# Linear attention with an MLP behind it: k turned by VectorE and DRAM, masks by ScalarE and GpSimd, TensorE in stated order

## The chip, the cores and the metric

The kernel runs on one core of a Trainium2 chip. The metric is the device time of one execution in microseconds, as a median of several executions. No run here fell in a slower state: each profile names the mean granted clock of TensorE, 0.97 to 1.00 of full speed in all of them, 0.995 before and 0.994 after.

## The reference, cut to what matters

```python
def _attn_ref(q, k, v, alpha):                     # (4, 8, 768, 48) each
    for t in range(S):
        state = alpha[:, :, t, :, None] * state + einsum('bhd,bhe->bhde', k[:, :, t], v[:, :, t])
        y[:, :, t] = einsum('bhd,bhde->bhe', q[:, :, t], state)

def _moe_ref(x, w_in, w_out):                      # 3072 tokens, 384 -> 2048 -> 384
    h = x @ w_in
    return (h * (1.0 / (1.0 + exp(-h)))) @ w_out   # x is y, heads side by side
```

## The kernel before: what the change and the argument touch

TensorE makes all matrix products here. They land in PSUM, in pieces called banks, from which ScalarE or VectorE has to take them before a bank can be used again. GpSimd does small work on the side, and SyncE issues DMAs.

The attention is done in 24 chunks of 128 tokens (6 per batch). In each, decayed k and q give scores, the scores are masked, masked scores and the state give values, and k with v gives the next state. The first 8 chunks are done with little beside them. In the 16 "late" ones, from the ninth on, the MLP's products of earlier tokens stand between the steps of a chunk; I call these *dense*. They use a scheme with fewer products and more sums, and the sums are VectorE's. VectorE also reads all weights and alpha once to prove that the scheme is safe; I call that the *guard*.

The late chunk, in the order of its stages (scores of the chunk before, then products, values and states, quotient):

```python
stages = [[(scores, 1)], [(products, 0)], [(values, 1), (states, 1)], [(quotient, 0), (blank, 0)]]

def scores(n):
    ps = c.pop("blank") if n >= NA else [ps_attn() for _ in range(2)]    # zeroed by ScalarE when late
    ...                                              # 32 products of 64 rows, the upper halves only
    for u in range(2):
        if n < NA:  ...                              # early: ScalarE copies, GpSimd selects
        m = mask[:, :, None, :]                      # late: VectorE multiplies by a mask
        dve.tensor_tensor(g[:, u]..., ps[u]..., m.to_broadcast(...), ALU.mult)
    if ci < NCH - 1:
        ps_k = ps_attn()
        for j in range(NP):
            pe.transpose(ps_k[:, j, :], c["kp"][:, j, :], ident)         # k for the state product
        c["kn"] = work.tile([128, NP, C], F32, name="kn")
        act.copy(c["kn"], ps_k)
```

Two more places carry the argument. `enter` makes the dense products of the first layer in three banks of PSUM; a bank is free again when ScalarE has copied it or VectorE has added it (`tt`), and the next product waits for that:

```python
def enter(grp, pair):
    ...
    add(a); tt(s[4], a, s[4])                        # VectorE frees bank a
```

`audit`, the guard, has one buffer: load, reduce for the maximum, reduce for the minimum (for the weights), next load, with VectorE's reductions kept in a stated order.

## Time and profile before

| kernel before | |
|---|---|
| time, median of the 3 runs made before the prediction | 561.52 us (561.36 to 562.27) |
| span of the profiled execution | 559.1 us |
| last product of TensorE ends at | 553.76 us |
| TensorE's waits after 127 us | two, 0.4 and 0.3 us |
| VectorE busy, 130 to 294 us | 145.6 of 164 us |
| VectorE busy, 450 to 517 us | 45.8 of 67 us |

The rows from which TensorE's and VectorE's load is read are in the prediction. The last two show where VectorE has room and where not. That the last stage has some did not make it safe, as the runs show.

### The profile page before, as it was taken

How to read it: one execution, taken by the hardware profiler on the slowest of the kernel's cores; microseconds unless marked ns; L12 is line 12 of the kernel's file. 1: busy time of each engine (PE TensorE's matmuls, PEld its weight loads, DVE VectorE, ACT ScalarE, POOL GpSimd, SP SyncE). 2: the span in 40 equal slices, each digit the busy share in tenths (PEclk: the TensorE clock that was granted, in tenths of full speed). 3: DMA queues.
4: the chain of work that ended last, by engine and by line, in shares of the span. 5: the costliest groups of instructions: out<-in, count | busy, mean ns of one | idle time of the engine just before them, and what ended most of it. 6: DMA issues, size and time to landing. Idle time of an engine off the chain costs nothing.

```text
span 559.1 us, 12435 instructions
## 1 busy us (share of the span) xinstructions
PE 543.4 (97%) x5074; PEld 492.6 (88%) x5074; DVE 448.1 (80%) x821; ACT 208.9 (37%) x414; POOL 20.8 (4%) x44
## 2 busy tenths in 40 slices
PE   5999999999999999999999999999999999999996
PEld 3788887898999999899989999999898999999995
DVE  5887789956998799986998897899895885857731
ACT  3456653323233342442433442443443342332100
POOL 5110000300000000000000000000000000000000
PEclk9899999999999999999999999999999999999999
DMA  9999871143443333333425444435422123334200
GB/s 208 223 288 201 235 187 42 26 118 100 101 107 97 82 86 88 98 87 86 130 69 162 141 113 133 131 81 154 132 69 88 53 84 118 101 98 122 72 30 26
DMA packets 94417, 63.81 MB, mean 114 GB/s; under 512 B 55312, under 2 KB 86032, under 8 KB 94352
## 3 DMA queue, kind: packets, MB, share of 16 engines
q1 hardware_dynamic: 94352, 62.94, 43.2%
q8 instruction: 41, 0.67, 0.5%
q14 instruction: 24, 0.20, 0.1%
HBM read 58.20 MB, written 4.72 MB: 113 GB/s over the span
## 4 chain that ended last, share of the span: by engine, by line
PE 79%; DVE 12%; DMA 3%; ACT 2%; SPq 1%; issue 1%; POOL 0%; DVEq 0%; ACTq 0%
PE ps_o L982 35%; PE ps_m L884 21%; PE ps_m L860 11%; PE ps_a L802 6%; PE ps_a L759 3%; PE ps_a L776 2%; DMA qn<-in_q_dram 1%; DVE g L898 1%; DMA bits<-in_moe_w_in_dram 1%; DVE u L701 1%; PE ps_a L817 1%; DVE p L730 1%; DVE seen L665 1%; SPq L456 1%; DVE w_out L626 1%
## 5 line engine op out<-in xcount | busy, mean ns | idle before, releaser
L982 PE MATMUL ps_o<-w_out,g 128*128 128x192 f32 x768 | 133.6, 328 | 0.0
L982 PEld LDWEIGHTS ps_o<-w_out,g 128*128 128x128 f32 x768 | 125.5, 190 | 2.7 <-issue 0.6
L982 PE MATMUL ps_o<-wt,g 128*128 128x192 f32 x576 | 100.0, 327 | 0.0
L982 PEld LDWEIGHTS ps_o<-wt,g 128*128 128x128 f32 x576 | 95.1, 190 | 1.5
L860 PE MATMUL ps_m<-xt,w_in 128*128 128x256 f32 x384 | 88.3, 382 | 0.8 <-ACT xt L807 0.8
L860 PEld LDWEIGHTS ps_m<-xt,w_in 128*128 128x128 f32 x384 | 71.1, 190 | 10.6 <-ACT xt L807 1.2
L884 PE MATMUL ps_m<-xc,w_in 128*128 128x256 f32 x288 | 70.1, 379 | 0.0
L884 PEld LDWEIGHTS ps_m<-xc,w_in 128*128 128x128 f32 x288 | 54.0, 190 | 6.4 <-DVE g L898 0.2
L665 DVE TENSOR_REDUCE seen<-bits 128x1 f32<-128x384 int32 (+2 forms) x65 | 42.4, 689 | 15.1 <-DMA bits<-in_moe_w_out_dram 14.9
L895 ACT ACTIVATE g<-g 128x1024 f32<-128x1024 f32 x32 | 33.1, 1055 | 56.5 <-DVE g L898 56.5
L987 DVE TENSOR_TENSOR g<-g 128x512 f32<-128x512 f32 x72 | 48.4, 685 | 6.0 <-PE ps_o L982 5.9
L890 ACT COPY g<-ps_m 128x512 f32<-128x512 f32 x64 | 36.7, 586 | 36.1 <-PE ps_m L884 36.0
L884 PE MATMUL ps_m<-xc,wx 128*128 128x256 f32 x192 | 50.1, 383 | 0.0
L782 ACT ACTIVATE st<-st,least 128x96 f32<-128x96 f32 x80 | 24.1, 364 | 57.3 <-DVE least L704 57.3
L884 PEld LDWEIGHTS ps_m<-xc,wx 128*128 128x128 f32 x192 | 35.0, 190 | 4.2 <-issue 0.4
L898 DVE TENSOR_TENSOR g<-ps_m,g 128x512 f32<-128x512 f32 x56 | 37.3, 681 | 0.7 <-PE ps_m L884 0.5
L701 DVE TENSOR_TENSOR_SCAN u<-al,one 128x516 f32<-128x516 f32 x24 | 29.1, 1211 | 8.7 <-POOL mask L535 4.5
L730 DVE TENSOR_TENSOR_SCAN p<-al,inv 128x516 f32<-128x516 f32 x24 | 29.4, 1225 | 5.2 <-PE ps_a L802 4.9
L863 ACT ACTIVATE g<-ps_m 128x512 f32<-128x512 f32 x32 | 19.0, 594 | 38.7 <-PE ps_m L860 38.6
L802 PE MATMUL ps_a<-g,vn 128*32 128x128 f32 x768 | 27.9, 281 | 1.8 <-POOL g L766 1.7
L802 PEld LDWEIGHTS ps_a<-g,vn 128*32 128x32 f32 x768 | 20.4, 111 | 9.1 <-issue 5.6
L890 ACT COPY part<-ps_m 128x512 f32<-128x512 f32 x32 | 18.6, 582 | 21.8 <-PE ps_m L884 17.6
(125 smaller groups left out, 632.1 us busy)
## 6 DMA issues: line engine op xcount, KB each, us to landing
bits<-in_moe_w_in_dram SPq DMA_DIRECT2D x24, 512.0 KB, 4.8
bits<-in_moe_w_out_dram SPq DMA_DIRECT2D x32, 384.0 KB, 3.3
at<-in_alpha_dram SPq DMA_DIRECT2D x64, 96.0 KB, 2.3
kt<-in_k_dram SPq DMA_DIRECT2D x64, 96.0 KB, 2.4
qt<-in_q_dram SPq DMA_DIRECT2D x64, 96.0 KB, 2.5
bits<-in_alpha_dram SPq DMA_DIRECT2D x9, 512.0 KB, 3.4
out_dram<-o SPq DMA_DIRECT2D x48, 96.0 KB, 1.7
an<-in_alpha_dram SPq DMA_DIRECT2D x8, 192.0 KB, 5.2
```

The lines of the kernel that those rows point to most:

```text
L665: dve.tensor_reduce(seen[kind][which][:, i : i + 1], x, axis=AX, op=op, apply_absolute_value=True))
L701: dve.tensor_tensor_scan(u[:, end - 1 :: -1], sg[:, end:0:-1], one[:, end:0:-1], 0.0, ALU.mult, ALU.add)
L730: dve.tensor_tensor_scan(p[:, 0:end], sg[:, 0:end], iv[:, 0:end], 0.0, ALU.mult, ALU.add)
L782: act.mul(s[:, j], s[:, j], least[:, n, j : j + 1])
L802: pe.matmul(py[32 * at : 32 * at + 32, t, :], lhsT=w, rhs=x, start=(i < 4), stop=(i >= len(todo) - 4), skip_group_check=True)
L860: pe.matmul(ps[:, e, :], lhsT=w_in[:, t, (f + e) * 128 : (f + e + 1) * 128], rhs=xt[:, t, :], start=(t == 0), stop=(t == NKT - 1))
L884: pe.matmul(ps[:, e], lhsT=block_w(w)[:, 2 * pair + e], rhs=block_x(grp, x), start=(first and e == 0), stop=(e == 1), skip_group_check=True)
L890: act.copy(to, ps)
L895: act.activation(x, x, AF.Silu)
L898: dve.tensor_tensor(to, a, b, op)
L982: pe.matmul(ps, lhsT=x, rhs=w[:, i], start=(first and i == 0), stop=(i == HF - 1), skip_group_check=True)
L987: dve.tensor_tensor(cells(grp, h, pair, *to), cells(grp, h, pair, *x), cells(grp, h, pair, *y), ALU.subtract)
```

## The change

Its intent: TensorE is the bound, so take the four transposes of k off it, and pay for the work on VectorE by taking the masks off VectorE. In parts:

1. k for the state product: VectorE transposes the 32x32 blocks (`flip`), SyncE writes the result to DRAM and reads it back with the blocks moved (`land`).
2. Masks: ScalarE copies the scores out of PSUM, GpSimd selects in place.
3. TensorE's instructions keep the order in which the program states them, from the ninth chunk on; the stages are reordered.
4. alpha, k and q are each fetched as soon as the tile is free; q's product gets a second buffer.
5. 40 of 48 output stores are issued by GpSimd.

```diff
+    def in_order(ins):
+        return tc.keep_in_program_order(ins) if late else ins
+    class pe:
+        def matmul(*args, **kw):
+            in_order(nc.tensor.matmul(*args, **kw))
 ...
-        p = turns(qps, n)
+        p = turns(qps if n < NA else [qps[0], late["p"]], n)
 ...
+    def flip(n):
+        if n < NA or c["ci"] == NCH - 1:
+            return
+        t = late["turn"].tile([128, NP, C], F32, name="turn").rearrange("p c (j d) -> p c j d", j=NP)
+        dve.transpose(t, c["kp"].rearrange("p j (c i) -> p c j i", i=32))
+        c["flip"] = dram.tile([128, NP * C], F32, name="flips")
+        nc.sync.dma_start(c["flip"], t.rearrange("p c j d -> p (c j d)"))
+    def land(n):
+        x = c.pop("flip").rearrange("(r d) (i x) -> i d r x", r=4, i=4)
+        for i in range(4):
+            nc.sync.dma_start(c["kn"][32 * i : 32 * i + 32], x[i])
 ...
-            m = mask[:, :, None, :]
-            dve.tensor_tensor(g[:, u]..., ps[u]..., m.to_broadcast(...), ALU.mult)
-        if ci < NCH - 1:
+            for u in range(2):
+                act.copy(swapped[:, :, u, :, CH:], ps[u][:, :, :, CH:])
+            for r, o in earlier:
+                for u in range(2):
+                    act.copy(swapped[r, o, u, :, 0:CH], ps[u][r, o, :, 0:CH])
+            for at, half in ((CH, later), (0, earlier)):
+                for r, o in half:
+                    gps.affine_select(x, x, pattern=[[0, NP], [1, CH]],
+                                      compare_op=ALU.is_ge, fill=0.0, base=0, channel_multiplier=-1)
+        if n < NA and ci < NCH - 1:
             ps_k = ps_attn()
 ...
-            nc.sync.dma_start(out[...], o)
+            (gps if grp < NG - 1 else nc.sync).dma_start(out[...], o)
 ...
-            stages = [[(scores, 1)], [(products, 0)], [(values, 1), (states, 1)], [(quotient, 0), (blank, 0)]]
+            stages = [[(land, 1), (scores, 1)], [(products, 0)], [(quotient, 0)],
+                      [(values, 1), (states, 1), (flip, 0)]]
```

What the diff does not show: the order of VectorE's and ScalarE's instructions is chosen by a scheduler, apart from a few that are pinned. Any edit, in the change or in an experiment, moves some of them.

More of the change, by code (lines that the diff above doesn't have):

```diff
@@ L376, in quotients, with transpose @@
     nc = tc.nc
-    pe, dve, act, gps = nc.tensor, nc.vector, nc.scalar, nc.gpsimd
+    dve, act, gps = nc.vector, nc.scalar, nc.gpsimd
+    late = {}
+    def in_order(ins):
+        return tc.keep_in_program_order(ins) if late else ins
+    class pe:
+        @staticmethod
+        def matmul(*args, **kw):
+            in_order(nc.tensor.matmul(*args, **kw))
+        @staticmethod
+        def transpose(*args):
+            in_order(nc.tensor.transpose(*args))
     B, H, S, D = q.shape
@@ L406, in quotients @@
     gpool = pool("gpool", 6)
-    opool = pool("opool", 2)
+    opool = pool("opool", 3)
     rpool = pool("rpool")
+    dram = pool("dram", 2, bass.MemoryType.DRAM)
     upool = pool("upool")
@@ L447, in quotients, with load @@
     ctxs = {}
-    def load(n):
+    def load(n, names="akq"):
+        if n == NT:
+            return
         c = ctxs.setdefault(n, dict(zip(("ci", "b"), divmod(n, B))))
@@ L452, in load @@
         for name, src in (("a", alpha), ("k", k), ("q", q)):
+            if name not in names:
+                continue
             x = src[b, :, rows, :]
@@ L517, in turns @@
     def turns(x, n):
-        return x[(n + 1) % 2 if n < NA else 0]
+        return x[(n + 1) % 2]
     one = consts.tile([128, NP * W + 1], F32, name="one")
@@ L526, in quotients @@
         gps.memset(t, 0.0)
-    mask = consts.tile([128, 2, C], F32, name="mask")
-    gps.memset(mask, 1.0)
-    for odd in range(2):
-        for e in range(2):
-            m = mask[CH * e : CH * e + CH, odd, :]
-            gps.affine_select(m, m, pattern=[[1, C]], compare_op=ALU.is_ge, fill=0.0,
-                              base=-CH * (e ^ odd), channel_multiplier=-1)
+    decayed = fix.tile([128, 2 * NP * C], F32, name="g")
+    low, high = slice(0, CH), slice(CH, C)
+    earlier, later = [(low, 0), (high, 1)], [(low, 1), (high, 0)]
+    ones = consts.tile([128, 1], F32, name="ones")
+    gps.memset(ones, 1.0)
     st = [fix.tile([128, NP, 2, D], F32, name=f"st{b}") for b in range(B)]
@@ L666, in audit @@
                                           apply_absolute_value=True))
-    xts, xcs, late = {}, {}, {}
+    xts, xcs = {}, {}
     def tokens(t):
@@ L687, in products @@
                     turned(c[name], tokens(sg))
+                    load(n + 1, "a")
                 continue
@@ L704, in products @@
         dve.tensor_single_scalar(least[:, n, :], u[:, 0:end:W], 2.0**-64, ALU.max)
-        kp = c["kp"] = turns(kps, n)
+        kp = c["kp"] = turns(kps, n) if n < NA else kps[0]
         ut = tokens(u)
@@ L709, in products @@
             turned(c["k"], ps["k"])
+            load(n + 1, "k")
         if n < NA:
@@ L734, in quotient @@
             turned(c["q"], q)
+            load(n + 1, "q")
         dve.tensor_tensor(qp, q, qp, ALU.mult)
-    def blank(n):
-        if n < NA:
+    def flip(n):
+        c = ctxs[n]
+        if n < NA or c["ci"] == NCH - 1:
             return
-        ps = ctxs[n]["blank"] = [ps_attn() for _ in range(2)]
-        for t in ps:
-            act.activation(t.rearrange("p j c -> p (j c)"), ident[:, 0:1].to_broadcast([128, 4 * C]),
-                           AF.Copy, scale=0.0)
+        t = late["turn"].tile([128, NP, C], F32, name="turn").rearrange("p c (j d) -> p c j d", j=NP)
[3 more added lines that the diff above has]
+    def land(n):
+        c = ctxs[n]
+        if "flip" in c:
+            c["kn"] = work.tile([128, NP, C], F32, name="kn")
+            x = c.pop("flip").rearrange("(r d) (i x) -> i d r x", r=4, i=4)
+            for i in range(4):
+                nc.sync.dma_start(c["kn"][32 * i : 32 * i + 32], x[i])
     def scores(n):
@@ L748, in scores @@
         ci, b = c["ci"], c["b"]
-        ps = c.pop("blank") if n >= NA else [ps_attn() for _ in range(2)]
+        ps = [ps_attn() for _ in range(2)]
         for j in (0, 2, 1, 3):
@@ L760, in scores @@
                               start=True, stop=True)
-        g = c["g"] = work.tile([128, 2, NP, C], F32, name="g")
-        for u in range(2):
-            if n < NA:
-                act.copy(g[:, u], ps[u])
-                gps.affine_select(g[:, u], g[:, u], pattern=[[0, NP], [1, C]], compare_op=ALU.is_ge,
-                                  fill=0.0, base=0, channel_multiplier=-1)
-                continue
-            m = mask[:, :, None, :]
-            dve.tensor_tensor(g[:, u].rearrange("p (o j) c -> p o j c", o=2),
-                              ps[u].rearrange("p (o j) c -> p o j c", o=2),
-                              m.to_broadcast([128, 2, NP // 2, C]), ALU.mult)
-        if ci < NCH - 1:
+        g = decayed.rearrange("p (u j c) -> p u j c", u=2, j=NP)
+        swapped = decayed.rearrange("p (o u j c) -> p o u j c", o=2, u=2, j=NP // 2)
+        c["g"] = (lambda u, j: g[:, u, j, :]) if n < NA else (
+            lambda u, j: swapped[:, j // 2, u, j % 2, :])
+        for u in range(2 if n < NA else 0):
+            act.copy(g[:, u], ps[u])
+            gps.affine_select(g[:, u], g[:, u], pattern=[[0, NP], [1, C]], compare_op=ALU.is_ge,
+                              fill=0.0, base=0, channel_multiplier=-1)
+        if n >= NA:
+            ps = [x.rearrange("p (o j) c -> p o j c", o=2) for x in ps]
+            for u in range(2):
[5 more added lines that the diff above has]
+                for r, o in half:
+                    x = swapped[r, o].rearrange("p u j c -> p (u j) c")[:, :, at : at + CH]
+                    gps.affine_select(x, x, pattern=[[0, NP], [1, CH]],
+                                      compare_op=ALU.is_ge, fill=0.0, base=0, channel_multiplier=-1)
+        if n < NA and ci < NCH - 1:
             ps_k = ps_attn()
@@ L781, in scores @@
             for j in range(NP):
-                act.mul(s[:, j], s[:, j], least[:, n, j : j + 1])
+                mul = act.mul(s[:, j], s[:, j], least[:, n, j : j + 1])
+                if late:
+                    tc.keep_in_program_order(mul)
     def values(n):
         c = ctxs[n]
-        ci, b, g, qp = c["ci"], c["b"], c["g"], c["qp"]
+        ci, b, g, qp = c["ci"], c["b"], c.pop("g"), c["qp"]
         vn = c["v"].rearrange("p (j u) d -> p j (u d)", u=2)
@@ L793, in values @@
         py = ps_attn()
-        todo = [(3 * j + i, vn[:, j, at : at + 32], g[:, u, j, :])
+        todo = [(3 * j + i, vn[:, j, at : at + 32], g(u, j))
                 for j in range(NP) for i, at, u in ((0, 0, 0), (1, 32, 0), (2, 80, 1))]
-        todo += [(3 * j + 1, vn[:, j, 48:80], g[:, 1, j, :]) for j in range(NP)]
+        todo += [(3 * j + 1, vn[:, j, 48:80], g(1, j)) for j in range(NP)]
         if ci > 0:
@@ L816, in states @@
                     r = slice(32 * i, 32 * i + 32)
-                    pe.matmul(ps[r, j, 0:D], lhsT=c["kn"][:, j, r], rhs=vn[:, 2 * j + i // 2, 0:D],
+                    kn = c["kn"][:, j, r] if n < NA else c["kn"][:, i, 32 * j : 32 * j + 32]
+                    pe.matmul(ps[r, j, 0:D], lhsT=kn, rhs=vn[:, 2 * j + i // 2, 0:D],
                               start=True, stop=True)
@@ L835, in sums_x @@
         for to, sa, a, sb, b in SUMS_X:
-            combine(block_x(grp, to), sa, block_x(grp, a), sb, block_x(grp, b))
+            tc.keep_in_program_order(
+                combine(block_x(grp, to), sa, block_x(grp, a), sb, block_x(grp, b)))
         yield
@@ L997, in store @@
             r = b * S + ci * C
-            nc.sync.dma_start(out[r : r + C, c * HO : (c + 1) * HO], o)
+            (gps if grp < NG - 1 else nc.sync).dma_start(out[r : r + C, c * HO : (c + 1) * HO], o)
         u1, u2, u3, u4 = [rpool.tile([128, HO], F32, name=f"u{j}") for j in range(4)]
@@ L1103, in quotients @@
     SLOTS = 4
-    marks = [2 * SLOTS + 2] + [(GB * i + 2 * GB) * SLOTS + 2 for i in range(len(phases))]
+    marks = [2 * SLOTS + 2] + [(GB * i + 2 * GB) * SLOTS + 3 for i in range(len(phases))]
     def settle():
@@ L1112, in settle @@
         quads = pool("quads")
+        late["p"] = pool("p").tile([128, NP * W + 1], F32, name="p")
         late["quads"] = {name: quads.tile([128, 32 + 4 * NP * D], F32, name=f"{name}t") for name in "akq"}
@@ L1155, in quotients @@
                     load(n + 1 + NIN)
-                if stage is quotient and n + 1 < NT:
-                    load(n + 1)
                 if stage is states and n + NV < NT:
                     load_v(n + NV)
+            if step * SLOTS + slot == (NA + 1) * SLOTS - 1:
+                x = decayed.rearrange("p (o i c) -> p o i c", o=2, c=C)
+                for r, o in later:
+                    gps.memset(x[r, o, :, 0:CH], 0.0)
             fill(step, slot)
@@ L1183, in quotients @@
     ps = ps_attn()[0:1, 0, 0:1]
-    pe.matmul(ps, lhsT=good, rhs=mask[:, 0, C - 1 : C], start=True, stop=True)
+    pe.matmul(ps, lhsT=good, rhs=ones, start=True, stop=True)
     dve.tensor_single_scalar(small, ps, 127.5, ALU.is_ge)
```

## The prediction

> **What bounds the kernel now.** I read four views in this order: the page's busy shares with the chain that ended last, the table of stretches, TensorE's own waits, and the timelines around one chunk. The page:
>
> ```profile
> PE 543.4 (97%) x5074; PEld 492.6 (88%) x5074; DVE 448.1 (80%) x821; ACT 208.9 (37%) x414; POOL 20.8 (4%) x44
> ...
> PE 79%; DVE 12%; DMA 3%; ACT 2%; SPq 1%; issue 1%; POOL 0%; DVEq 0%; ACTq 0%
> ```
>
> TensorE is busy 97% and weight loads 88%; GpSimd is nearly unused, and VectorE is second at 80%. Is TensorE full in the stage that the change touches (chunks 8 to 23, about 127 us on)? The table of stretches (length, then busy us and instruction count per engine, granted clock, DMA share, GB/s):
>
> ```profile
> 130.00:212.00 82.00, 82.00 (x950) 74.46 (x952) 71.49 (x137) 29.14 (x65) 0.00 (x0) 1.00 0.39 99
> 212.00:294.00 82.00, 81.26 (x803) 73.87 (x791) 74.09 (x134) 33.34 (x65) 0.00 (x0) 1.00 0.34 92
> 360.00:450.00 90.00, 89.99 (x853) 81.98 (x852) 79.18 (x144) 36.83 (x68) 0.00 (x0) 1.00 0.35 97
> 554.00:559.20 5.20, 0.00 (x0) 0.00 (x0) 0.15 (x1) 0.00 (x0) 0.00 (x0) 0.79 0.08 25
> ```
>
> There TensorE (first pair after the length) is never without a matmul except 0.74 us in the second stretch; VectorE is at 87 to 90%; DMA is a third used. What TensorE waited for in the whole run:
>
> ```profile
> PE ps_m L884 <- DVE g L898: 0.4, 1, 0.4
> PE ps_m L884 <- ACT g L890: 0.3, 1, 0.3
> ```
>
> These two rows are that 0.74 us and the only waits of the late stage; the other eight rows (4.0 us and less) belong to the first 127 us. So a late instruction off TensorE that is removed gives nothing by itself, and one removed from TensorE gives its whole issue time. The 12% VectorE in the chain is partly an artefact: the chain steps over to an engine that was just in time, while TensorE was running.
>
> The removed TensorE work can be measured in this trace, because the last four chunks already go without it. A chunk with transposes, then one without:
>
> ```profile
> 148.63 0.90 PE L759 MATMUL ps_a<-p,kp 48*64 48x128 f32 x32
> ...
> 149.46 0.66 PE L776 MATMUL ps_a<-ident,kp 128*128 128x128 f32 x4
> ...
> 149.95 2.75 PE L860 MATMUL ps_m<-xt,w_in 128*128 128x256 f32 x12
> ```
>
> ```profile
> 392.13 0.90 PE L759 MATMUL ps_a<-p,kp 48*64 48x128 f32 x32
> 392.96 2.87 PE L982 MATMUL ps_o<-w_out,g 128*128 128x192 f32 x16
> ```
>
> From the first score to the next dense product: 149.95 - 148.63 = 1.32 us with four transposes, 392.96 - 392.13 = 0.83 us without. Difference 0.49 us per chunk.
>
> **What the Trainium skill says.** "Perfetto Trace Analysis", Identifying the Most-Contended Engine, warns that matmul busy share is a poor measure, since matmuls are pipelined, and prefers weight-load busy. I therefore used starts: 8 products of L982 start to end in 2.6 us again and again, so the stream really is dense; agrees. "VectorE: DVE Perf Modes", The three transpose paths: VectorE transposes only inside 32x32 blocks. So its new transpose of k cannot do what TensorE's did, and the trip through DRAM moves the blocks; the trace of before shows only the duration of such an instruction, 1109 ns for 128x512. "SBUF — State Buffer", Who interferes with whom: GpSimd shares a port pair with VectorE, as an exclusive lock; a VectorE instruction with two SBUF inputs and a GpSimd instruction that reads SBUF block each other. The trace agrees:
>
> ```profile
> 15.54 0.69 DVE L627 CUSTOM_DVE_ANT_0 w_in<-w_in,up 128x1024 uint16<-128x1024 uint16 x1
> ...
> 19.21 1.67 POOL L766 TENSOR_SCALAR_AFFINE_SELECT g<-g 128x512 f32<-128x512 f32 x2 [4.82 <-ACT g L765]
> 19.32 1.07 DVE L627 CUSTOM_DVE_ANT_0 w_in<-w_in,up 128x1024 uint16<-128x1024 uint16 x1
> ```
>
> The same VectorE instruction takes 0.69 us alone and 1.07 beside a mask by GpSimd. "DMA: Bandwidth & Descriptors", Two DMAs through the same engine are not ordered: a DMA that reads what another wrote must wait for its completion. So the read of flipped k waits on the SyncE queue; no trace of before shows such a pair.
>
> **The change part by part.** It acts on the 16 late chunks.
>
> 1. TensorE loses the four transposes of k in every late chunk that still updates a state: chunks 8 to 19, 12 of them (the row has 80 = 20 x 4 transposes, 32 of them early). 12 x 0.49 = 5.9 us, all on the path.
> 2. VectorE loses the mask product, two of 0.683 us per chunk (row L770, x32): 16 x 1.37 = 21.9 us. It gains one block transpose, taken as 1.11 us like the other stream transposes: 12 x 1.11 = 13.3 us. Net -8.6 us, none of it on the path by itself.
> 3. ScalarE loses two zero fills (L743, 0.599) and one copy of k (L778, 0.588): 1.79 us per chunk. It gains two copies of 256 and four of 128 elements per partition. From its copies out of PSUM (128x512 0.586, 128x192 0.315) I estimate 0.15 us + 0.85 ns per element: 2 x 0.37 + 4 x 0.26 = 1.78 us. Even. But the six copies, and the four state scalings behind them (4 x 0.364), now stand in one block of 3.2 us right after the scores, before copies that free banks of the dense products.
> 4. GpSimd gains four selects per chunk. The early select of 512 elements takes about 0.63 us when nothing is beside it (half of a run like the 1.67 above, less the blocking), so 256 should take 0.33: 1.3 us per chunk plus blocking by VectorE. In the worst case VectorE loses 1.3 us per chunk to the lock, more than it saved in 2 per chunk (1.37 - 1.11 = 0.26): from 88% to about 93%. GpSimd also issues 44 of the 48 output stores.
> 5. k through DRAM adds 256 KB out and 256 KB in per chunk, 12 x 0.5 = 6.3 MB on 63.8. A 96 KB load lands about 2.4 us after issue (issue table); two trips one behind the other plus five issues of 0.5 us are an estimated 7 to 8 us. Time for it: from the kp product at 139.3 us to this chunk's state update near 156.9 us was 17 us before, and the new order puts the update later still. Hidden.
> 6. Order. In the comparison of instruction orders, the steady chunk of before had 4 or 5 dense groups (2.6 us each) between scores and values; after, there are 6, with one group between values and next scores. So masks get about 15.6 us; part 3's copies and part 4's selects need 1.8 + 1.3 + up to four waits of about 0.7 to 1.2 us, at most 8 us. Hidden. In the first late chunks (8 to 11) there are only 4 groups, 10.4 us: tight for chunk 8, which also waits for two memsets of the mask tile behind three stores on GpSimd. The second buffer for p lets the q product run before the previous values, so the next scores should not wait for VectorE.
> 7. Fetching alpha, k, q as their tiles come free: earlier loads, no TensorE wait names a load in the late stage, so nothing gained.
>
> Sum: -5.9 (part 1), -0.4 (I count half of the two 0.3 to 0.4 us waits as gone), +0.3 (a small new wait at chunk 8 or behind part 3's block): -6.0 us. 561.5 - 6.0 = 555.5; I take 555.4. The early 127 us and the last 37 us of pure output products are unchanged. GpSimd's start loses the making of the mask (0.31 + 1.29 us), but the start's chain runs through loads of q, so that is free.
>
> **Rivals.**
>
> A. VectorE or the lock takes over: for it, 88 to 90% busy before, more blocking after, and the two late waits are both for evacuation work. Against it: the sum leaves 7%, and every product group has slack of a group. It would show as TensorE waits for VectorE or ScalarE of 0.3 to 0.5 us in most chunks: +4 to +6 us, time 559 to 562.
>
> B. A new wait at the handover of masks or k: values waiting for GpSimd, or states for the DRAM trip, because SyncE's queue is in order and stands behind a slow load. Six groups of slack speak against it; in chunk 8 to 11 it is possible, a few us once: 556 to 559.
>
> C. More than the transposes comes off: the fixed order also removes turnarounds or early idle (66 to 130 us has 1.2 us without a matmul). Ceiling, all late and mid waits gone: 5.9 + 0.7 + 1.2 = 7.8 us, 553.7. A 2% gain needs 11.2 us, which TensorE does not have to give.
>
> **Range and chances.** Centre 555.4; low 552.5 (rival C and some luck in the start), high 559.5 (A halfway or B). Eight in ten between. Faster by over 2% (below 550.3) 4%, within 2% 93%, slower 3% (only if A and B act together through every chunk).
>
> **What would show it.** Right: TensorE busy near 537 us with a share still 97%; L776's successor with 32 transposes only; 0.83 us from scores to the next dense product in all late chunks; late waits of TensorE under 1 us in sum; new VectorE transpose x12 near 1.1 us; selects of 0.3 to 1.3 us with VectorE instructions stretched beside them. Wrong: a late TensorE wait for GpSimd's mask tile, for a load of kn, or repeated waits for VectorE's or ScalarE's evacuations, with TensorE's share under 96%; or the start longer or shorter by more than 1 us.

## The result, and the profile after

| | before | after |
|---|---|---|
| time, median of 4 runs each | 561.89 us (561.36 to 562.32) | 559.96 us (559.79 to 560.61) |
| span of the profiled execution | 559.1 | 558.1 |
| last product of TensorE ends at | 553.76 | 553.50 |

The ratio is 0.9968, with a 95% interval of 0.9951 to 0.9985. Ratios here are the mean time of one kernel's fast runs over the mean of the other's in the same rounds, so not quite the ratio of the medians. The predicted 555.4 us was 4.6 us too low, and 559.96 lies just above the range's end of 559.5.

All TensorE instructions now have one line, that of a helper (L388, transposes L392), so they are told apart by their tiles. The page of the kernel after:

```profile
PE 541.4 (97%) x5026; PEld 488.8 (88%) x5026; DVE 445.1 (80%) x801; ACT 208.4 (37%) x466; POOL 75.9 (14%) x146
```

48 instructions fewer on TensorE, as expected, but 2.0 us less busy instead of 6. Its waits in the late stage, all for VectorE (total us, times, longest):

```profile
PE ps_m L388 <- DVE g L944: 1.3, 2, 0.9
...
PE ps_m L388 <- DVE xc L586: 1.0, 1, 1.0
PE ps_o L388 <- DVE o L1042: 0.9, 2, 0.7
...
PE ps_a L388 <- DVE p L758: 0.5, 1, 0.5
```

3.7 us in six places, where before had 0.7 us in two. The table of stretches shows where (columns as in the prediction, GpSimd after ScalarE):

```profile
130.00:212.00 82.00, 81.52 (x947) 74.07 (x939) 69.77 (x130) 28.87 (x82) 13.74 (x25) 1.00 0.44 118
212.00:294.00 82.00, 80.65 (x768) 73.19 (x767) 77.45 (x135) 34.93 (x81) 12.23 (x24) 1.00 0.47 127
294.00:360.00 66.00, 66.00 (x742) 60.49 (x741) 58.12 (x98) 25.56 (x59) 9.90 (x19) 1.00 0.57 154
360.00:450.00 90.00, 88.98 (x772) 81.12 (x771) 73.90 (x132) 38.47 (x89) 13.66 (x24) 1.00 0.35 95
450.00:517.00 67.00, 66.22 (x358) 61.65 (x356) 45.51 (x87) 20.79 (x33) 4.31 (x8) 1.00 0.34 112
```

Each stretch but one has a hole on TensorE of 0.5 to 1.4 us. In the second, VectorE is busy 77.45 of 82 us, where it had been 74.09.

**What the transposes were worth.** A chunk of the kernel after, from its scores on (start, length):

```profile
300.81 2.87 PE L388 MATMUL ps_o<-w_out,g 128*128 128x192 f32 x16
303.51 1.03 PE L388 MATMUL ps_m<-xc,wx 128*128 128x256 f32 x4
```

A run of 16 such products takes 2.76 us where it follows other dense work and 2.87 here. Instruction by instruction, start to start: the first one after the scores takes 267 ns, the others 162 or 163. Behind the scores in the kernel before stood the transposes, with 166 ns for the first and 109 for the other three, and then the dense products at their usual pace. So the four transposes took 493 ns, and 105 ns of that comes back at the first dense product: 0.39 us per chunk instead of 0.49. The Trainium skill says in "TensorEngine Tiling (Array Packing)", Key Properties, that changing the tiling mode drains TensorE, without a figure. The trace agrees in kind: the scores use 48x64 tiles, what follows 128x128, and behind the switch the first instruction of the new kind takes longer with either follower, 57 ns for a transpose and 105 ns for a dense product. But the switch is not all there is to it: a dense product that has waited takes the same 104 ns more with no change of tile (four products of 256 columns in 1.13 us after the wait shown next, in 1.03 us otherwise). So this is what TensorE pays here for starting again, after a switch or after a wait. The prediction counted it as part of the transposes.

**The largest wait.** TensorE of the kernel after at 218 us (idle before, and what ended it, in brackets):

```profile
214.72 2.87 PE L388 MATMUL ps_o<-w_out,g 128*128 128x192 f32 x16
217.42 1.03 PE L388 MATMUL ps_m<-xc,wx 128*128 128x256 f32 x4
219.37 1.13 PE L388 MATMUL ps_m<-xt,wx 128*128 128x256 f32 x4 [0.92 <-DVE g L944]
```

It wants a bank which VectorE has to add out of PSUM first. VectorE, and GpSimd's selects beside it:

```profile
212.56 0.71 DVE L768 STREAM_TRANSPOSE turn<-kp 128x512 f32<-128x512 f32 x1
...
213.96 0.42 DVE L582 TENSOR_TENSOR w_in<-w_in 128x256 f32<-128x256 f32 x1
214.30 0.42 DVE L582 TENSOR_TENSOR w_in<-wx 128x256 f32<-128x256 f32 x1
214.75 0.42 DVE L586 TENSOR_TENSOR w_in<-w_in 128x256 f32<-128x256 f32 x1
215.09 0.42 DVE L582 TENSOR_TENSOR w_in<-wx,w_in 128x256 f32<-128x256 f32 x1
215.43 1.11 DVE L696 STREAM_TRANSPOSE al<-at 128x512 f32<-128x512 f32 x1
216.37 0.71 DVE L868 TENSOR_TENSOR st<-ps_a,st 48x192 f32<-48x192 f32 x2
217.11 1.49 DVE L722 TENSOR_TENSOR_SCAN u<-al,one 128x516 f32<-128x516 f32 x1
218.62 0.69 DVE L944 TENSOR_TENSOR g<-ps_m,g 128x512 f32<-128x512 f32 x1
```

```profile
215.68 1.84 POOL L813 TENSOR_SCALAR_AFFINE_SELECT g<-g 64x256 f32<-64x256 f32 x4 [10.00 <-ACT g L806]
```

No line has idle time in brackets: VectorE works without a pause, and the addition for which TensorE stands comes ninth of those shown. k's block transpose is one of the eight ahead of it, and the scan takes 1.49 us instead of 1.23, with the selects beside its start.

**The end.** The last stretch was not changed, yet TensorE waits there too. TensorE and VectorE of the kernel after:

```profile
515.68 3.25 PE L388 MATMUL ps_o<-w_out,g 128*128 128x192 f32 x16 [0.71 <-DVE o L1042]
```

```profile
513.75 1.00 DVE L685 TENSOR_REDUCE seen<-bits 128x1 f32<-128x384 int32 x2
514.67 0.68 DVE L587 SCALAR_TENSOR_TENSOR g<-g 128x512 f32<-128x512 f32 x1
515.27 0.35 DVE L1042 TENSOR_TENSOR o<-ps_o,u 128x192 f32<-128x192 f32 x1
```

The sum o is behind two reductions of the guard. TensorE's order in this stretch is the same in both kernels, two one-column products of a check apart. In the kernel before it was some 2 us later relative to these reductions, and passed without a wait.

**The whole of it on TensorE**, from the time between the starts of its instructions, less the usual pace of each kind:

| term | before to after |
|---|---|
| 12 x 4 transposes gone, less the late first product (12 x 0.39) | -4.7 us |
| from scores to values, 16 chunks: time over the usual 1.69, now 3.48 | +1.8 |
| from values to the next scores: 0.08, now 0.55 | +0.5 |
| after the last values (442 us on): 2.19, now 4.10 | +1.9 |
| before the first late scores | +0.3 |
| sum; measured at TensorE's last product: 553.76 to 553.50 | -0.2; -0.26 |

The span gained 0.76 us more after TensorE's last product (5.35 us before, 4.60 after), which makes the 1.0 us between the two profiles. The medians differ by another 0.9 us that this pair of profiles does not show.

The new work itself, in the groups of instructions of the kernel after (count, busy us, mean ns):

```profile
L813 POOL TENSOR_SCALAR_AFFINE_SELECT g<-g 64x256 f32<-64x256 f32 x64 | 34.2, 534 | 124.8 <-ACT g L806 105.8 <-ACT g L809 15.8
L809 ACT COPY g<-ps_a 64x128 f32<-64x128 f32 x64 | 13.7, 264 | 0.4
L806 ACT COPY g<-ps_a 128x256 f32<-128x256 f32 x32 | 10.4, 376 | 10.0 <-PE ps_a L388 10.0
L768 DVE STREAM_TRANSPOSE turn<-kp 128x512 f32<-128x512 f32 x12 | 8.5, 708 | 0.1
```

ScalarE's copies are as estimated. The block transpose takes 0.71 us instead of the assumed 1.11. VectorE's late work fell by 9.3 us in sum, from 389.3 to 380.0, although 33 of its instructions are now stretched, by 5.4 us together, 4.2 of it beside GpSimd.

### The profile page after: what moved, and what is told of

It is laid out like the page before. It is cut to its first block, busy times and chain, and to the rows that moved or that the text cites. A ratio compares the mean times of both kernels' runs of the same rounds, so it can differ in the third digit from the quotient of the medians.

```text
span 558.1 us, 12640 instructions
## 1 busy us (share of the span) xinstructions
PE 541.4 (97%) x5026; PEld 488.8 (88%) x5026; DVE 445.1 (80%) x801; ACT 208.4 (37%) x466; POOL 75.9 (14%) x146
## 5 line engine op out<-in xcount | busy, mean ns | idle before, releaser
L388 PE MATMUL ps_o<-w_out,g 128*128 128x192 f32 x768 | 134.7, 329 | 1.1 <-DVE o L1042 0.9
L388 PEld LDWEIGHTS ps_o<-w_out,g 128*128 128x128 f32 x768 | 125.4, 190 | 5.1 <-DVE o L1042 2.3
L388 PE MATMUL ps_m<-xt,w_in 128*128 128x256 f32 x480 | 113.6, 383 | 1.5 <-ACT xt L851 1.1
L388 PEld LDWEIGHTS ps_m<-xt,w_in 128*128 128x128 f32 x480 | 89.1, 190 | 14.4 <-ACT xt L851 1.6
L388 PE MATMUL ps_o<-wt,g 128*128 128x192 f32 x576 | 99.7, 326 | 0.0
L388 PEld LDWEIGHTS ps_o<-wt,g 128*128 128x128 f32 x576 | 95.1, 190 | 1.6 <-issue 0.2
L388 PE MATMUL ps_m<-xc,w_in 128*128 128x256 f32 x288 | 70.7, 382 | 0.0
L388 PEld LDWEIGHTS ps_m<-xc,w_in 128*128 128x128 f32 x288 | 53.6, 190 | 7.0 <-DVE g L944 0.3
L1033 DVE TENSOR_TENSOR g<-g 128x512 f32<-128x512 f32 x72 | 49.8, 708 | 6.1 <-PE ps_o L388 6.1
L1045 POOL DMA_DIRECT2D out_dram<-o x40 | 22.0, 550 | 223.2 <-DVE o L1042 127.6
L813 POOL TENSOR_SCALAR_AFFINE_SELECT g<-g 64x256 f32<-64x256 f32 x64 | 34.2, 534 | 124.8 <-ACT g L806 105.8
L388 PE MATMUL ps_m<-xc,wx 128*128 128x256 f32 x192 | 50.0, 383 | 1.0 <-DVE xc L586 1.0
L388 PEld LDWEIGHTS ps_m<-xc,wx 128*128 128x128 f32 x192 | 35.2, 190 | 5.3 <-ACT u L1064 1.3
L388 PE MATMUL ps_a<-g,vn 128*32 128x128 f32 x768 | 27.5, 278 | 1.8 <-POOL g L801 1.7
```

What stands on the lines that cost most here:

```text
L388: in_order(nc.tensor.matmul(*args, **kw))
L813: gps.affine_select(x, x, pattern=[[0, NP], [1, CH]], compare_op=ALU.is_ge, fill=0.0, base=0, channel_multiplier=-1)
L1033: dve.tensor_tensor(cells(grp, h, pair, *to), cells(grp, h, pair, *x), cells(grp, h, pair, *y), ALU.subtract)
L1045: (gps if grp < NG - 1 else nc.sync).dma_start(out[r : r + C, c * HO : (c + 1) * HO], o)
```

## The experiments

My theory after the result: TensorE's gain is real but is given back to waits for VectorE, because a change that shortens TensorE everywhere leaves VectorE, at about 90% in the middle stage, as a second limit (rival A of the prediction, in a few places instead of most chunks). The rivals: the new order on TensorE makes the waits; the transposes were never worth much; the masks' or k's handover costs.

Each experiment is an edit of the kernel after, except the one named. All are timed in five rounds against the kernel before. The runs fall into four sets, in which the kernel before had medians of 560.98 to 562.04 us: compare ratios, not times, between sets. An edit that takes work away mostly lets the scheduler place VectorE's rest anew, so a difference of a few tenths of a per cent between two of them is not all due to what was taken away. Where the traces show the order unchanged, I say so.

### k on TensorE again

```diff
 def flip(n):
-        if n < NA or c["ci"] == NCH - 1:
+        if True:
             return
-        if n < NA and ci < NCH - 1:
+        if ci < NCH - 1:
             ps_k = ps_attn()
```

> The changed kernel with one part undone: k of the late chunks is again transposed by TensorE and copied by ScalarE; no block transpose, no trip through DRAM. Theory 1 (the removal was worth less than the 5.9 us of the prediction, because the first dense matmul after scores now pays the change of weights that the transposes used to pay): accounting of both traces gives 0.395 us per chunk, 12 x 0.395 = 4.7 us, so 559.96 + 4.7 = 564.7 us, less up to 1.5 us if VectorE, relieved of 12 x 0.71 us, waits less: 563 to 565. Theory 2 (the removal is worth 5.9 us and the new waits have nothing to do with k): 565.9. Theory 3 (the trip of k itself causes the new waits): 560 to 561.

Measured: correct, 562.48 us (561.5 to 564.87), ratio 1.0029 (1.0015 to 1.0043). Undoing k's move costs 0.6%, about 3.4 us. In microseconds this is between the ranges of the theories, but the kernel before was faster in this set (560.98 us) than in the one that the ranges were reckoned from (561.89 us). As ratios, theory 1's 563 to 565 us are 1.002 to 1.0055, so 1.0029 is theory 1. The 0.1 us behind the transposes is shown above; that a change of weights is its cause, as the text has it, is not. More telling is that the rest of the change is then slower than the kernel before.

### The masks on VectorE again

```diff
-            for u in range(2):
-                act.copy(swapped[...], ps[u][...]) ...
-                    gps.affine_select(x, x, ...)
+            for u in range(2):
+                dve.tensor_tensor(g[:, u]..., ps[u]..., mask..., ALU.mult)
+    (with the two zero fills by ScalarE, as before)
```

> The changed kernel with the masks back on VectorE (two products of 0.68 us and two zero fills by ScalarE in each late chunk, as before), the rest as changed. Theory 1 (VectorE's backlog): 16 x 1.37 = 22 us more work there and so more waits, 1 to 4 us slower than the changed kernel: ratio to the kernel before 0.9985 to 1.004. Theory 2 (the lock or GpSimd): 1 to 2 us faster, 0.993 to 0.995. Theory 3 (neither): 0.9955 to 0.998.

Measured: correct, 562.8 us (561.82 to 565.78), ratio 1.0018 (1.001 to 1.0026). Theory 1: 22 us more work on VectorE cost about 2.8 us. TensorE's waits in this kernel:

```profile
PE ps_m L388 <- DVE g L952: 2.5, 6, 0.7
PE ps_o L388 <- DVE o L1050: 2.3, 4, 1.3
```

### Both moves undone

Both edits together: what stays is the order, the loads, the second buffer and the stores.

> The changed kernel with both moves of work undone: k is transposed on TensorE again (48 transposes) and the masks are products on VectorE again. What stays of the change is TensorE's stated order, the earlier loads, the second p buffer and the stores issued by GpSimd. So far: k undone alone 1.0029, masks undone alone 1.0018 of the kernel before, both done 0.9968. Theory 1 (the stated order with a loaded VectorE costs; the two moves each buy back about 3 us, and add up): 1.0029 + 1.0018 - 0.9968 = 1.008, so 1.006 to 1.010, 564.5 to 567.5 us. Theory 2 (the rest of the change is neutral, the two moves merely overlap in what they save): 0.998 to 1.003.

Measured: correct, 564.03 us (562.4 to 565.18), ratio 1.0028 (1.0017 to 1.0039): theory 2, and the sum that theory 1 expected is not there. The four kernels make a square:

| ratio to the kernel before | masks on VectorE | masks on ScalarE and GpSimd |
|---|---|---|
| k on TensorE | 1.0028 | 1.0029 |
| k on VectorE and through DRAM | 1.0018 | 0.9968 |

Moving the masks alone is worth nothing: VectorE gets free time while TensorE is the limit. Moving k alone is worth 0.1%, which is within the noise (the intervals are about 0.001 to either side): TensorE gets free time, which VectorE takes. Both together are worth 0.6%, 3.4 us. And what is left of the change without them costs 0.3%.

### The transposes taken away from the kernel before

This one alone is an edit of the kernel before, with a wrong result on purpose.

```diff
-        if ci < NCH - 1:
+        if n < NA and ci < NCH - 1:
             ps_k = ps_attn()
 ...
-                    pe.matmul(ps[r, j, 0:D], lhsT=c["kn"][:, j, r], rhs=vn[...])
+                    pe.matmul(ps[r, j, 0:D], lhsT=(c["kn"][:, j, r] if n < NA else ident[:, r]), rhs=vn[...])
```

> The kernel before with nothing changed but the removal: the late chunks' four transposes of k on TensorE and ScalarE's copy of them are left out and the state products read a constant instead (a wrong result on purpose). It measures the term of 5.9 us by itself. Theory 1 (a chunk's transposes are worth 0.395 us, because the dense group behind them takes back 0.1 us): 12 x 0.395 = 4.7 us off, ratio to the kernel before 0.991 to 0.9925. Theory 2 (0.49 us as the prediction had it): 5.9 us, ratio 0.989 to 0.9905. Theory 3 (any shortening of TensorE is eaten by VectorE, whatever the rest of the change does): ratio 0.994 to 0.998, with new TensorE waits of 2 us or more for VectorE.

Measured: 559.63 us (559.2 to 560.38), ratio 0.9961 (0.9948 to 0.9975). That is theory 3: 2.2 us for 48 transposes, less than half of their 4.7. Of 12 x 0.39 us on TensorE, part comes back as waits for VectorE (2.3 us in the late stage, where it had been 0.4) with nothing new on VectorE or GpSimd at all:

```profile
PE ps_a L759 <- DVE p L735: 0.9, 2, 0.6
...
PE ps_o L982 <- DVE o L996: 0.7, 2, 0.4
PE ps_m L884 <- DVE g L898: 0.7, 2, 0.4
```

So the kernel before, with its two small waits, was already close to VectorE's limit, and the prediction's 5.9 us were not there to be had by taking work from TensorE.

### k's transposes on VectorE and the trip through DRAM taken away

A wrong result on purpose: `flip` returns at once, and the state products read a constant.

> The changed kernel without k's new way: no block transpose on VectorE (12 x 0.71 us less there) and no trip through DRAM; the state products read a constant (a wrong result on purpose). Theory 1 (the new waits are VectorE's backlog, and the transposes are part of it): the waits near 218 us shrink from 0.9 to under 0.4, and the whole is 1 to 2 us faster than the changed kernel: ratio to the kernel before 0.993 to 0.995. Theory 2 (the transposes are beside the point): as the changed kernel, 0.9955 to 0.998.

Measured: 560.5 us (559.34 to 561.23), ratio 0.9972 (0.9963 to 0.9982): theory 2 by the number. 8.5 us less on VectorE gained nothing by themselves. The wait near 218 us did not shrink, as theory 1 would have it, but grew: in the new placing, VectorE had another scan and another transpose ahead of the addition.

```profile
218.34 1.13 PE L388 MATMUL ps_m<-xt,wx 128*128 128x256 f32 x4 [1.20 <-DVE g L944]
```

### GpSimd's selects taken away

A wrong result on purpose: the late `affine_select` is left out, ScalarE's copies stay.

> The changed kernel without GpSimd's four selects in each late chunk (a wrong result on purpose); ScalarE's copies stay. Theory 1 (rival A by the lock: stretched VectorE instructions, 5.4 us in all, make the new waits): stretched instructions fall under 1.5 us, the waits of TensorE for VectorE fall from about 4 us to about 2, ratio to the kernel before 0.992 to 0.995. Theory 2 (VectorE's order and its plain backlog): as the changed kernel, 0.9955 to 0.998.

Measured: 558.28 us (557.8 to 558.69), ratio 0.9936 (0.9922 to 0.9949): theory 1, 1.8 us faster than the changed kernel. Stretched VectorE instructions fell from 5.4 to 0.4 us, and from scores to values TensorE lost 1.8 us less. Another placing is excluded: TensorE, VectorE and ScalarE have the same instructions in the same order in both traces (5026, 801 and 466). No late wait of TensorE in the kernel after names the selects, so what they cost goes through VectorE, by the stretching.

The size is less sure than the cause. TensorE's late waits for VectorE fell only from 3.7 to 3.1 us, not to the 2 us of theory 1, because those for the sums o grew from 0.9 to 1.9 us. Of the 1.7 us between the two profiled spans, 0.9 us lies before the first late scores, where nothing was removed. So the profiles give 0.9 us for the selects, and the timings 1.8 us, give or take 1.2.

### The guard's reductions of the weights taken away

The result stays right; the proof that it will be is incomplete, so this is no version to keep.

```diff
+        todo = [x for x in todo if x[2] == 0]          # alpha alone
```

The test of what these reductions found is left out at the end of the kernel too.

> The changed kernel without the 56 reductions that check the exponents of the weights (the guard is weaker, the result is the same): VectorE has about 31 us less to do, all after chunk 12, and the loads behind them are gone. If VectorE's backlog makes TensorE's waits, those at 479 and 515 to 517 us go for sure (1.5 us) and the others shrink: 556.5 to 558.5. If only the lock or the fixed order does: 559.5 or more.

Measured: 558.62 us (558.6 to 559.22), ratio 0.9956 (0.9943 to 0.9969), 0.7 us faster than the changed kernel. The two intervals overlap, so this alone is not clear of the noise, though about 31 us of work left VectorE. In its profile the waits between 478 and 517 us are gone, one of 0.5 us at 532 us is new, and that at 218 us is as before.

### Selects and guard taken away; then k's transposes too

Wrong results on purpose, combinations of the edits above.

> The changed kernel without GpSimd's selects in the late chunks and without the guard's reductions of the weights (a wrong result on purpose). Alone these gave 0.9936 and 0.9956, against 0.9968 for the changed kernel. Theory 1 (both burden VectorE in different stretches, and what they cost TensorE adds): 0.991 to 0.993, waits of TensorE for VectorE after 130 us under 1.5 us. Theory 2 (a delay that one causes hides the other's): 0.9932 to 0.9950.

Measured: 557.23 us (556.54 to 557.89), ratio 0.9923 (0.991 to 0.9936). Theory 1: 0.9968 less 0.0032 (selects) less 0.0012 (guard) is 0.9924, so they add, as far as intervals of 0.001 to either side can tell. TensorE's late waits for VectorE are 1.6 us, just over the 1.5 of theory 1. With the run without the guard this is a second pair that differs by the selects alone: the orders of TensorE, VectorE and ScalarE are again the same, and the selects cost 0.0033, 1.9 us (1.7 us between the profiles, from the first late scores to TensorE's last product).

> The same, and without k's block transposes on VectorE and its trip through DRAM too (a wrong result on purpose). Theory 1 (VectorE is the whole of the miss): all late waits gone but 1 us, 0.988 to 0.991, which is the predicted 555.4 or a little over. Theory 2 (something else keeps the rest): 0.991 to 0.994.

Measured: 555.79 us (554.86 to 556.16), ratio 0.9889 (0.9874 to 0.9903), theory 1, which is the predicted time. k's transposes with their trip, worth nothing alone, are worth 0.34% once the other two are gone. That the time equals the predicted one is in part luck: by the ratio it is 6.2 us under the kernel before, while the transposes are worth 4.7, and the kernel before has the guard too and was not run without it. The stretches of this kernel:

```profile
130.00:212.00 82.00, 82.00 (x942) 74.49 (x933) 67.88 (x130) 28.76 (x82) 2.70 (x5) 1.00 0.36 91
212.00:294.00 82.00, 81.18 (x778) 73.74 (x780) 74.83 (x133) 34.69 (x81) 4.32 (x8) 1.00 0.45 118
...
360.00:450.00 90.00, 90.00 (x778) 82.25 (x778) 60.77 (x113) 38.07 (x88) 4.31 (x8) 1.00 0.13 33
450.00:517.00 67.00, 67.00 (x368) 63.02 (x367) 32.04 (x55) 21.65 (x34) 4.31 (x8) 1.00 0.04 13
```

TensorE is full again, but for 0.8 us in the second row (and a wait of 0.5 us at 530 us), and its order is that of the changed kernel, the two products of the check apart. So the stated order does not by itself make the waits: with less on VectorE, the same order runs dense.

### TensorE's order left to the scheduler

```diff
-        return tc.keep_in_program_order(ins) if late else ins
+        return ins
```

> The changed kernel without the stated order of TensorE (the scheduler places its instructions as in the kernel before); both moves of work stay. Theory 1 (a fixed order costs, because TensorE then stands at a sum that VectorE is late with instead of taking what is ready): 1.5 to 4 us faster than the changed kernel, ratio to the kernel before 0.989 to 0.994. Theory 2 (the order helps or is neutral; the waits are VectorE's backlog wherever TensorE stands): 0.9955 or more, up to 1.001.

Measured: correct, 573.26 us (571.55 to 575.44), ratio 1.0191 (1.0177 to 1.0204). Both theories fell: without the stated order the kernel is 12 us slower. The scheduler, left to itself, puts TensorE behind VectorE's and ScalarE's work far more often:

```profile
PE ps_o L388 <- DVE o L1042: 3.1, 4, 1.4
PE ps_m L388 <- ACT part L936: 1.8, 1, 1.8
PE ps_m L388 <- DVE xc L582: 1.5, 3, 0.6
```

### VectorE in stated order too

Every VectorE instruction from the ninth chunk on is kept in program order, as TensorE's.

> The changed kernel with VectorE's instructions too in the order in which the program states them, from the ninth chunk on. Theory 1 (the six waits come from the scheduler's interleaving on VectorE, sums of weights and alpha's scan ahead of a bank that TensorE waits for): fewer waits, ratio 0.990 to 0.995. Theory 2 (VectorE has too much to do there in any order): 0.9955 to 1.003.

Measured: correct, 589.7 us (587.2 to 591.28), ratio 1.0492 (1.0471 to 1.0514), beyond both theories. TensorE waits 11.5 us for the sums o and 7.8 for g. The order in which this program states VectorE's work is no order to run it in; whether another one would do better than the scheduler's stays open.

### More work on GpSimd: two runs that measured something else

Eight more instructions of half the selects' size (64x128) per late chunk on a tile that nobody else uses any more, once selects (which read), once fills (which only write), to tell a lock on reads from one on writes.

```diff
+                    for y in (ident[r], ident[r]):
+                        gps.affine_select(y, y, ...)        # or: gps.memset(y, 0.0)
```

> The changed kernel with eight more small selects per late chunk on GpSimd, which read and write a tile that nobody needs any more; the order on TensorE, VectorE and ScalarE is the same instruction by instruction. If the lock between GpSimd reads and VectorE is what makes VectorE late: VectorE's stretched time grows from 5.4 us to 8 to 12 us, TensorE's late waits grow by 1 to 3 us, time 561 to 563. If VectorE's order and load alone make the waits: within 0.4 us of 559.96.

> Control for the run with more selects: eight memsets of the same tile in their place, which write but read nothing. Lock theory: no more stretching of VectorE than in the changed kernel (5.4 us), time within 0.4 us of 559.96. If it were the mere time of GpSimd (a later mask), it would slow as much as the selects do.

Measured: 592.1 us, ratio 1.055 (1.0536 to 1.0564), and 572.97 us, ratio 1.0211 (1.0198 to 1.0225). Neither says anything of a lock. The extra instructions depend on nothing late, so all 128 were done on GpSimd ahead of the first late masks, nearly in one run, and TensorE waited once. The first of the two:

```profile
PE ps_a L388 <- POOL g L813: 31.6, 1, 31.6
```

592.1 less 31.6 is 560.5, the changed kernel; in the second the wait is 12.6 us, and 572.97 less 12.6 is 560.4. An added cost has to be tied to the place where it is to act.

### Stores by SyncE, the guard earlier, the guard's loads by GpSimd

Three attempts at a better kernel, each a line's edit: all stores issued by SyncE; `step > 2 * GB + 2` instead of `3 * GB + 2`; `gps.dma_start` for the guard's loads.

> The changed kernel with all output stores issued by SyncE again, as before. Theory 1 (the stores' queue has no part): 0.9958 to 0.998. Theory 2 (GpSimd's issues of 0.55 us each delay masks or free the o tiles late): 1 us or more faster, under 0.995. Theory 3 (SyncE's queue needed the relief: the loads and k's trip stand behind stores that wait for their sums): 0.999 to 1.005, with TensorE or VectorE waits for DMA.

> The changed kernel with the guard reductions of VectorE begun four chunks earlier, so that they are done before the last output products. Without them at all the kernel ran at 0.9956. Theory 1 (the reductions between 478 and 517 us make those 1.1 us of TensorE's waits, and VectorE has room for them before): waits at 514 to 517 us gone, 0.9945 to 0.9962. Theory 2 (VectorE between 212 and 360 us is full, so they only move the waits): 0.9962 to 1.000, with longer waits at 218 to 300 us.

> The changed kernel with the guard's loads issued by GpSimd instead of SyncE. Theory 1 (VectorE stands 15 to 20 us for these loads because they wait in SyncE's queue, which makes TensorE's last waits): 0.9945 to 0.996. Theory 2 (one buffer sets their pace, whichever queue issues): 0.996 to 0.9985. Theory 3 (they now hold up GpSimd's masks): over 0.999 with TensorE waits for GpSimd.

| | time, us | ratio to the kernel before |
|---|---|---|
| stores by SyncE | 564.23 | 1.0045 (1.0033 to 1.0057) |
| guard four chunks earlier | 567.9 | 1.0106 (1.0091 to 1.012) |
| guard's loads by GpSimd | 571.07 | 1.0158 (1.0143 to 1.0174) |

All three are correct and slower. The first has theory 3's number, and its sign on VectorE but hardly on TensorE: VectorE waits 31.4 us for the guard's loads, where it had been 24.0, and TensorE 0.2 us for k's trip. TensorE mostly stands for VectorE, in more places than in the changed kernel. VectorE's order differs as well, TensorE's does not, so the loads are not shown to be the whole cause. The second moved the waits, as theory 2 says, but to an unexpected place, rival B of the prediction:

```profile
PE ps_a L388 <- DMA kn<-flips: 3.7, 3, 2.3
PE ps_a L388 <- DMA kt<-in_k_dram: 2.1, 1, 2.1
```

k's trip shares the SyncE queue with the guard's loads, and its slack is smaller than it looked. The third has theory 3's number and not its sign either: 6.1 us of waits for the sums g, the longest 2.1 us, none for the late masks. VectorE waits longer for the guard's loads than before the edit, 31.6 us for those of the weights against 24.0, so giving them another queue did not help them. None of the correct kernels beats the changed one with its guard whole.

## Why the prediction was wrong, point by point

- **TensorE is the bound in the late stage, and what leaves VectorE alone gives nothing.** Right: the masks' move makes no difference while k is on TensorE (1.0029 against 1.0028). One reading beside it was wrong, and nothing rests on it: "8 products of L982 start to end in 2.6 us" are 16 products, 163 ns from start to start.
- **"one removed from TensorE gives its whole issue time".** Wrong, and the main failure. Taken from the kernel before, the transposes gave 2.2 us instead of 5.9. The step that failed is the overlap: it took VectorE's work to stay hidden behind a shorter TensorE. Two waits of 0.4 and 0.3 us in some 430 us showed only that VectorE was just in time, not that it had room; with only the transposes and ScalarE's copy of them taken away, TensorE waited 2.3 us for VectorE.
- **Part 1, 12 x 0.49 = 5.9 us.** Mis-sized: 0.39, so 4.7 us. What TensorE pays for starting again behind the scores' small tiles was counted as part of the transposes; it stays and falls to the next product (105 ns).
- **Part 2, VectorE -8.6 us.** Right in sum, -9.3, but by luck: the transpose was cheaper than assumed (0.71, not 1.11: 4.8 us less), and the stretched instructions took that back.
- **Part 3, ScalarE even.** Right for the copies: 0.376 and 0.264 us against 0.37 and 0.26. No late wait for ScalarE's block of copies appeared.
- **Part 4, selects and lock.** A select takes 0.53 us instead of 0.33, and 0.41 where nothing with two inputs runs beside it. Beside the selects VectorE lost 4.2 us, 0.26 us per chunk, a fifth of the worst case. The prediction charged it to VectorE's share and not to the path. The run without selects puts 0.9 us (profiles) to 1.8 us (timings) on the path. GpSimd issues 40 stores, not 44.
- **Parts 5 and 6, handovers hidden.** Right in this kernel: no late wait names the masks or k's trip, and 0.83 us from scores to the next dense product holds in all late chunks. SyncE did stand for the first trip to land before it issued the read (seven times, 5.7 us in all), without TensorE noticing. The margin of k's trip is thin: guard loads four chunks earlier broke it. The order was taken as a mere rearrangement. It is a condition: without it, 12 us more.
- **Part 7, earlier loads.** Not tested alone; no wait speaks for or against.
- **The sum's -0.4 and +0.3.** The term that failed: new waits, and the slower starts behind them, came to +4.5 us (the four positive rows of the table), where the prediction had -0.1 net. Rival A had the time (559 to 562) but the wrong shape: not 0.3 to 0.5 us in most chunks, but 0.5 to 1.0 us in a few places where VectorE's long instructions bunch ahead of a bank, a score's operand or an output sum. It was argued away with "the sum leaves 7%". A mean over a stretch says nothing of the six microseconds ahead of one bank.

That VectorE is what kept the gain is shown by the run of the kernel before without the transposes, where TensorE's new waits are mostly for VectorE, and by the last of the combined runs, 0.9889, where TensorE runs dense in the same order. The selects' part, 0.9 to 1.9 us, is free of the scheduler's placing. That they stretch VectorE is measured; that the stretching is the lock which the prediction took from the skill fits, but no run isolates it. For the rest, how much is amount of work and how much the placing is not settled: the run without k's transposes has less work and the same time. The combined runs also took away the guard's loads and k's trip, which share a DMA queue, so that VectorE's instructions alone are not isolated there. Why the remainder of the change costs 0.3% is open too; in its profile TensorE stands for VectorE near 216 us and after 480 us.

## What to carry to other kernels

A bound engine that waits almost nowhere may still have a second engine right behind it: before counting a removal as its whole time, look at how long ahead of its use each result of the second engine was ready, above all where that engine's instructions are long and bunched. Move work off both together, because either move alone may be worth nothing, and check by taking the second engine's burdens away, even with wrong results, whether the first then runs dense. When removed instructions stood next to a change of tile size, take the pace of the instruction that follows as part of the comparison.

## What the Trainium skill lacked or had wrong

- "TensorEngine Tiling (Array Packing)", Key Properties, says that a change of tiling mode drains TensorE, with no figure: here, from 48x64 tiles to 128x128, the first of the dense fp32 products of 192 columns took 105 ns more than the next, and the first of the fp32 transposes 57 ns more. Behind a wait, with no change of tile, the first dense product took 104 ns more too, so the figure is not of the switch alone.
- "VectorE: DVE Perf Modes", The three transpose paths, has one time, for 128x128 bf16. Here fp32 128x512 took 0.71 us in k's layout and 1.11 us in that of the alpha, k and q tiles, so the layout counts.
- "SBUF — State Buffer", Who interferes with whom, agrees in kind: VectorE's late instructions, mostly those with two SBUF inputs, were stretched by 5.4 us, 4.2 of it beside the 64 selects, and by 0.4 us without them. For what the selects lose themselves it has no figure: 0.53 us on average against 0.41 alone.
- No page has the time of a select on GpSimd (0.41 us for 64x256 fp32 alone).
